# Zero pads written as 16 bit elements, and a new hand-held issue order, in a one-core linear attention and gated convolution kernel

## The chip, the cores and the metric

The kernel runs on one core of a Trainium2 chip. The metric is device microseconds of one execution. A core has a matrix engine (TensorE, PE in the profile), three elementwise engines (VectorE or DVE, ScalarE or ACT, GpSimd or POOL), a queue engine (SyncE, SP) and 16 DMA engines. Each engine takes its instructions strictly in its own order; engines meet through semaphores.

## The reference, cut to what matters

For 8 batches, 8 heads, 576 positions and a head size of 64, a linear attention is computed, its output is laid out as (position, 512), and a gated convolution follows:

```python
r = np.maximum(x, 0.0)                       # phi for q and k
phi = np.concatenate([r * cos_w, r * sin_w], axis=-1)
kv  = einsum('bhsf,bhsd->bhfd', k_p, v);  z = sum(k_p, axis=2)
att = einsum('bhsf,bhfd->bhsd', q_p, kv) / (einsum('bhsf,bhf->bhs', q_p, z) + 1e-06)
x1, x2, x3 = split(att @ w_proj)             # 512 -> 3 * 512
x2_conv = irfft(rfft(x2) * rfft(filter_fft)) # over the 576 positions
out = (x1 * x2_conv * x3) @ w_out            # 512 -> 512
```

## The kernel before

Everything is held in fp16 with fp32 accumulation in PSUM. One batch is one pass through these named steps; a step is a Python generator, and each `yield` in it ends one piece:

- `Lq`, `Lk`, `Lv` (line 278 and 285) load a batch of q, k or v from HBM into one of six `raw` tiles over POOL's DMA queue, as two transfers: partitions 0 to 63 take five positions each, partitions 64 to 127 take four. `Sk` loads the first half of k of batch 0 over SP's queue into a tile that shares its memory with `att`. Half 0 and 1 of batch 0 are loaded apart. `Lw`, `Lf`, `Lo` load `w_proj` in three thirds, the filter and `w_out`.
- Since the upper 64 partitions have four positions and the lower have five, the fifth place of the upper ones is zeroed once in each `raw` tile: `pad:0` to `pad:5` (step_pad, line 358), on DVE. `pd32` does it for the fp32 tile (line 362).
- `cols`, `rows`, `tf`, `ti`, `th`, `io`, `id`, `sine`, `zero` build the tables of sines and masks. `ccol`, `scol`, `tcol` are the weights of phi.
- `pk`, `pq`, `va` make phi(k), phi(q) and the scaled v, in pieces on DVE (line 249) or ACT (lines 605 and 477). `kv` (line 654) and its eviction `kvs`, `qt` (transposes of q: on PE, line 675, for batches 0 to 2, as DMA transposes on SP, line 666, from batch 3), `num` (line 689, then `rcp` at line 699 and `att` on DVE), `xp` or `xt` (transposes of `att`, line 721 on PE, line 711 on SP).
- `ga` and `gb` are the x1 and x3 matmuls with `w_proj` (line 858), evicted to `x0s` and `x2s`, multiplied in `g`. `bf`, `pr`, `dm`, `dr`, `dl`, `xe`, `pd`, `inv`, `y` are the convolution by a factored transform (lines 769 to 895). `out` (line 937 and 943) is the last product; its result is scaled into one of three `os` tiles (line 268) and stored by SP (lines 969 and 959).

No scheduler orders the work: `PLAN` is a text of words such as `pq:0.1'a*3`, each word advances one step by one piece (`*3`: three pieces; `'a`: this piece on ACT, `'v`: on DVE, in place of the step's own engine), and each engine gets its instructions in the order of the text. A `~` ahead of a load holds it until the last scalar or tensor operation that DVE had been given in the text is done. `UNITS` is a text of digits: which of the four PSUM tiles each new unit takes. Waits between engines are derived by the framework from the tiles that instructions read and write. POOL builds the descriptors of its transfers itself, some 0.65 to 0.75 us for each.

step_pad writes its zeros through an fp32 view of the fp16 tile:

```python
nc.vector.memset(raw_buf[i].bitcast(FP32)[64:128, :, 2 * D : 5 * D // 2], 0.0)
```

Of the kernel before, what the change touches and what calls it, by code (L numbers as in the profile page):

```python
# [10 lines left out]
FP32 = mybir.dt.float32  # L11
# [16 lines left out]
    num:0.1 rows: va:0.1 pq:0.1'a pk:0.1*2 num:0.0 num:0.1 pq:0.1 num:0.1 tf:0 qt:0.2 num:0.0  # L28
    pk:0.1'a tf:1 qt:0.3 rows: va:0.1 num:0.1 rows: pk:0.1 pq:1.2 pk:0.1'a qt:0.2 kv:0.1
    pq:1.2'a num:0.0 kv:0.1 ~Lw:0.0.4 pq:1.2'a qt:0.3'v xp:0.0*2 ti: pq:1.2 num:0.2 num:0.3  # L30
    pq:1.2 num:0.2 tf:0 pq:1.2 num:0.2 num:0.3 va:1.2'v qt:1.3 Lk:1.2 num:0.3 qt:1.2 va:1.2'v
    num:0.2 num:0.3 qt:1.3'v qt:1.0 qt:1.2 xp:0.1 Lw:1.0.4 va:1.2 ti: xp:0.1'v gb:0.1 qt:1.0
    qt:1.1 bf:0.0 ti: bf:0.1 gb:0.0 bf:0.0 gb:0.0 va:1.2'v qt:1.1'v tf:0 gb:0.1 Lv:2.2 ga:0.1*2
# [12 lines left out]
    pd:0.1 pq:3.2 gb:1.2 kv:2.2 gb:1.1 num:2.0 bf:1.0 qt:2.3 pd:0.0 gb:1.1 gb:1.2 bf:1.1 gb:1.1
    inv:0.3 num:2.0 pq:3.2*2 gb:1.2 num:2.0 inv:0.3 inv:0.1 num:2.0 g:1.1 inv:0.2 bf:1.1 inv:0.1
    inv:0.2 bf:1.1 num:2.1*2 gb:1.3 num:2.1 pq:3.2 va:3.2 gb:1.3 inv:0.0 gb:1.3 bf:1.0 Lk:4.2
    pr:1.1 num:2.1 pq:4.2 g:1.2 inv:0.0 xp:2.0 bf:1.1 num:2.2 bf:1.0 y:0.5 pr:1.1 num:2.2
    num:2.3 va:3.2 y:0.5 xp:2.0 num:2.2 pq:3.2'a pr:1.1 bf:1.1 pq:3.2'a bf:1.0 pq:4.2 pr:1.0*2  # L50
    va:4.2 num:2.3 num:2.2 pr:1.2 num:2.3 pk:3.2 pr:1.2 ga:1.3*2 num:2.3 xp:2.1 pr:1.0 dm:1.1
    va:3.2'v pq:4.2 ga:1.3 bf:2.0 dm:1.0 xp:2.1 dr:1 ga:2.0 y:0.5*2 ga:2.0 pk:3.2 y:0.4 xe:1.0
    pk:3.2 va:3.2'v Lo: y:0.5 y:0.4 dl:1 ga:2.0 xe:1.2 gb:2.1 gb:2.0 va:4.2'v xe:1.1 y:0.4*2
    g:1.3 ga:2.1 gb:2.1 y:0.4 bf:2.1 pk:3.2 pd:1.2 gb:2.0 ga:2.1 bf:2.0 qt:3.2 va:3.2 gb:2.1
    out:0.1 pd:1.2 Lv:5.2 gb:2.0 pk:3.2'a*2 gb:2.2 pd:1.2 out:0.1 bf:2.1 g:2.0 kv:3.2 bf:2.0
    pd:1.2*2 kv:3.2 ~Lq:5.2 va:4.2 ga:2.1 qt:3.1 out:0.1 pk:4.2 gb:2.2 qt:3.3 ga:2.2 kv:3.2
    bf:2.1*2 bf:2.0 ga:2.2 gb:2.2 bf:2.1 out:0.2 bf:2.0 va:4.2 pk:4.2 g:2.1 inv:1.0 pq:4.2
# [12 lines left out]
    inv:2.1'v inv:2.2 y:2.4 num:4.1 qt:5.0 inv:2.3 inv:2.2 pr:3.0 num:4.1 y:2.4 inv:2.3 pk:5.2'a  # L70
    pr:3.1 va:5.2 num:4.1 gb:3.2 y:2.4 pr:3.1 pk:5.2'a num:4.1 num:4.2 pr:3.0'v kv:5.2*2 g:3.1
    bf:3.2 gb:3.2 qt:5.1 pr:3.1 y:2.4 y:2.5 num:4.2 y:2.5 kv:5.2 pr:3.2 num:4.2 num:5.0 y:2.4
    gb:3.2 num:4.2 dm:3.1 pr:3.2 num:5.0 num:5.3 num:5.0*2 dm:3.0 num:5.3 dr:3 num:5.3*2
    ga:3.3*2 va:6.2'v y:2.5 gb:3.3 xe:3.1 gb:3.3 xe:3.0 xt:4.0 ga:3.3 xt:4.1 gb:3.3 pk:6.2 y:2.5
    qt:5.2 num:5.1 dl:3 ~Lq:6.2 num:5.1 xe:3.2 num:5.1 g:3.2 pd:3.2 ga:4.0 gb:4.0 num:5.1 ga:4.1
    ga:4.0 y:2.5 pd:3.2 gb:4.0 va:6.2 ga:4.0 gb:4.0 ga:4.1 g:3.3 num:5.2 out:0.1 bf:4.2 gb:4.1
    out:2.0 num:5.2 g:4.0 num:5.2*2 gb:4.1 out:2.0 gb:4.2 ga:4.1 xt:5.0 gb:4.1 pd:3.2*2 gb:4.3
    bf:4.2 gb:4.2 bf:4.2*2 ga:4.2 ~Lq:7.2 out:2.0 g:4.1 gb:4.2 pd:3.2 gb:4.3*2 ga:4.3*2 ga:4.2
    pq:6.2 ga:4.3 inv:3.2 xt:5.1 inv:3.3 inv:3.0 ga:4.2'v g:4.3 inv:3.3 out:1.0 inv:3.2 bf:4.2
    inv:3.1 pk:6.2'a g:4.2 out:2.0 pk:6.2 bf:4.2 bf:5.2 out:1.2 ga:5.1 pr:4.0 pq:6.2 pk:6.2  # L80
    pk:6.2'a ga:5.1 inv:3.1 y:3.5 pr:4.0 bf:4.2 pr:4.1*2 y:3.5 inv:3.0 va:6.2 out:2.1 bf:4.2
# [6 lines left out]
    bf:5.2 gb:5.0 out:3.1 gb:5.0 inv:4.1 qt:6.0 bf:5.2 inv:4.2 pk:7.2 y:4.4 gb:5.0 y:4.4 num:6.1
    inv:4.2 num:6.1 pr:5.2 out:3.2 y:4.4 pr:5.2 qt:6.2 qt:6.3 num:6.1 g:5.1 gb:5.3 num:6.0
    out:3.2 va:7.2 g:5.0 gb:5.3 num:6.1 num:6.0 gb:5.3 ga:5.3*2 num:6.2 num:6.0*2 inv:4.3 ga:5.3  # L90
    pk:7.2 pr:5.1 num:6.3 num:6.2 inv:4.3 pr:5.1 num:6.2 y:4.4 num:6.2 num:6.3 gb:5.2*2 num:6.3
    va:7.2'v num:6.3 dm:5.0 pr:5.1 y:4.5*3 out:3.2 dm:5.1 dr:5 gb:5.2 dl:5 ga:5.2 xt:6.0 y:4.5
# [955 lines left out]
```

## Time and profile before

| what | value |
| --- | --- |
| median of 3 runs | 236.4 us (235.6 to 236.49) |
| the profiled execution | 235.66 us, of which the span of its instructions is 233.9 us |
| PE matmuls | 205.8 us busy, 88% of the span, 2260 instructions |
| DVE | 199.4 us busy, 85%, 573 instructions |
| ACT | 174.1 us busy, 74%, 266 instructions |
| POOL | 43.7 us busy, 19% |
| mean granted TensorE clock | 0.962 |

The profiled execution lies 0.74 us below the median, and 1.76 us of it are outside the span. Busy time merges overlapping instructions of an engine: a DVE instruction of 0.34 us may start 0.26 us after the one before. A matmul's end is modelled, so that a PE that is shown busy need not be at its peak. L numbers are lines of the kernel, and many share the line of a helper: L249 is any scalar operation on DVE, L254 any tensor operation, L268 any eviction on ACT.

### The profile page before, as it was taken

Reading aid. Unit: us, or ns where it says so; the run is one execution under the profiler, and the core shown is the slowest. Engines: PE = TensorE matmul, PEld = TensorE weight load, DVE = VectorE, ACT = ScalarE, POOL = GpSimd, SP = SyncE. Lnnn points to the kernel's source line nnn. Section 1 sums busy time; section 2 is a strip of 40 time slices with the busy share of each in tenths; the row PEclk is TensorE's granted clock in tenths of the full one; section 3 lists DMA queues with packets and bytes.
Section 4 is the critical chain, followed back from the end, with each engine's and each line's share of the span. In section 5 each row is a group of like instructions: output and inputs, shape, how many; then the busy total and the mean of one; then the engine's idle time right before and its main releaser. Section 6 shows DMA issues by size and latency. Waiting matters only on the chain.

```text
span 233.9 us, 5838 instructions
## 1 busy us (share of the span) xinstructions
PE 205.8 (88%) x2260; PEld 135.9 (58%) x2260; DVE 199.4 (85%) x573; ACT 174.1 (74%) x266; POOL 43.7 (19%) x80
## 2 busy tenths in 40 slices
PE   0380599999999999998699999999999999999990
...
DVE  1480889999999999989479999999999799989960
...
PEclk9998579999999999999799999999999999999996
...
GB/s 130 106 156 189 201 202 150 0 130 200 168 174 201 201 160 119 137 202 199 162 144 152 189 185 201 226 197 153 131 150 226 190 170 154 114 0 7 108 219 185
DMA packets 73115, 36.78 MB, mean 157 GB/s; under 512 B 41152, under 2 KB 68800, under 8 KB 73088
## 3 DMA queue, kind: packets, MB, share of 16 engines
...
q14 instruction: 10, 0.08, 0.1%
...
## 4 chain that ended last, share of the span: by engine, by line
PE 76%; DMA 7%; issue 5%; DVE 5%; ACT 4%; SPq 1%; ACTq 1%; POOL 0%; DVEq 0%; POOLq 0%
PE ps L858 27%; PE ps L769 12%; PE ps L937 8%; DMA out_dram<-os 4%; PE ps L689 4%; PE ps L654 4%; PE ps L891 3%; PE ps L895 3%; PE ps L791 3%; DMA raw<-in_q_dram 2%; PE ps L675 2%; PE ps L778 2%; PE ps L721 2%; PE ps L802 2%; ACT os L268 1%
## 5 line engine op out<-in xcount | busy, mean ns | idle before, releaser
L858 PE MATMUL ps<-xt,wp 128*128 128x320 f16 (+1 forms) x512 | 72.8, 289 | 0.0
L858 PEld LDWEIGHTS <-wp 128*128 128x128 f16 x512 | 48.3, 99 | 17.7 <-issue 2.5
L937 PE MATMUL ps<-wo,y 128*128 128x512 f16 x128 | 31.3, 379 | 0.0
L769 PE MATMUL ps<-wp,fo 128*128 128x512 f16 x128 | 31.1, 379 | 0.0
L268 ACT ACTIVATE os<-ps 128x1024 f32<-128x1024 f32 (+1 forms) x21 | 16.9, 812 | 12.7 <-PE ps L937 7.5
L254 DVE TENSOR_TENSOR att<-ps,rcp 128x640 f16<-128x640 f32 x32 | 25.9, 819 | 0.2
L268 ACT ACTIVATE x2f<-ps 128x1024 f16<-128x1024 f32 (+1 forms) x23 | 19.7, 873 | 7.3 <-PE ps L769 6.8
L689 PE MATMUL ps<-kvs,qpt 128*128 128x65 f16 x320 | 14.8, 197 | 10.6 <-DVE qpt L266 6.5
L268 ACT CAST x2s<-ps 128x576 f16<-128x576 f32 x29 | 18.5, 647 | 4.9 <-PE ps L858 2.7
L689 PEld LDWEIGHTS <-qpt 128*128 128x128 f16 x320 | 13.7, 100 | 13.8 <-DVE qpt L266 6.6
L268 ACT CAST x0s<-ps 128x576 f16<-128x576 f32 x29 | 18.4, 645 | 3.9 <-PE ps L858 2.9
L268 ACT CAST eq<-ps 128x576 f16<-128x576 f32 x28 | 17.1, 653 | 3.8 <-PE ps L895 3.6
L937 PEld LDWEIGHTS <-y 128*128 128x128 f16 x128 | 12.0, 98 | 13.0 <-DVE y L254 1.0
L268 ACT CAST xf<-ps 128x1024 f16<-128x1024 f32 (+1 forms) x21 | 16.0, 809 | 3.8 <-PE ps L802 3.4
L769 PEld LDWEIGHTS <-fo 128*128 128x128 f16 x128 | 11.9, 98 | 11.0 <-issue 0.4
L254 DVE TENSOR_TENSOR eo<-eq 128x512 f16<-128x512 f16 (+1 forms) x72 | 16.8, 285 | 0.5
L477 ACT ACTIVATE va<-raw,ccol 128x512 f16<-128x512 f16 (+1 forms) x25 | 17.1, 688 | 0.0
L891 PE MATMUL ps<-itab,yf 128*128 128x144 f16 x128 | 16.9, 229 | 0.0
L895 PE MATMUL ps<-itl,yf 128*128 128x288 f16 x64 | 16.9, 291 | 0.0
L278 POOL DMA_DIRECT2D raw<-in_q_dram x9 | 6.4, 708 | 51.6 <-ACT x2s L268 19.7
L254 DVE TENSOR_TENSOR g<-x0s,x2s 128x576 f16<-128x576 f16 x32 | 14.0, 444 | 1.6 <-ACT x0s L268 1.5
L254 DVE TENSOR_TENSOR eo<-xt 128x512 f16<-128x512 f16 (+3 forms) x44 | 15.1, 367 | 0.0
...
## 6 DMA issues: line engine op xcount, KB each, us to landing
...
```

The source lines that it names most:

```text
L254: last_dve[0] = nc.vector.tensor_tensor(out=out, in0=in0, in1=in1, op=op)
L268: return nc.scalar.copy(out=out, in_=in_) if mul is None else nc.scalar.mul(out=out, in_=in_, mul=mul)
L278: first = queue.dma_start(out=rw[0:64, to], in_=rows[:, :, 0 : NJ * D])
L477: return nc.scalar.activation(out=dst, in_=src, func=AF.Copy if bias is None else AF.Identity, scale=col, **({} if bias is None else {"bia ...
L654: nc.tensor.matmul(u[:, g, ds((h % 4) * 65, 65)], kp[:, h, j].rearrange("p a b -> p (a b)"), va[:, h, j, 0:65], start=(j == 0), stop=(j == ...
L689: nc.tensor.matmul(u[:, hh, ds(t * 65, 65)], qpt[:, h, ds(t * 128, 128)], kvs[:, h // 4, ds((h % 4) * 65, 65)], start=True, stop=True,)
L769: nc.tensor.matmul(u[:, x], fo[:, bl, c, x], wp[c], start=(c == 0), stop=(c == NC - 1),)
L791: nc.tensor.matmul(u[:, comp], tab[:, ds(128 * bl + 32 * comp, 128)], x2f[:, cl], start=True, stop=False,)
L858: nc.tensor.matmul(uf[:, ds(512 - 64 * NJ * (1 - hf), 64 * n)], wp16[:, i, ds(w * DM + c * 128, 128)], xi[:, hf, 0:n], start=(i == 0), sto ...
L891: nc.tensor.matmul(u[:, comp, ds(par * QS, QS)], yf[:, comp, ds(par * DM + c * 128, 128)], itab[:, par + 4 * comp], start=(par == 0), stop ...
L895: nc.tensor.matmul(u[:, comp, 0:HS], yf[:, comp, 2 * DM : NF], itl[:, c, comp].rearrange("p a b -> p (a b)"), start=False, stop=True,)
L937: nc.tensor.matmul(u[:, x], y[:, c, ds(128 * t, 128)], wo16[:, c], start=(c == 0), stop=(c == NC - 1),)
```

## The change

The zeros of step_pad are written through the tile's own 16 bit view. Both texts, `PLAN` and `UNITS`, are replaced: the order of the pieces, the engine of some, the places of the loads and of the holds, and the PSUM tile of each unit. Nothing else differs. Below: the edited line, the head of the two plans, and the stretch around the stores of batches 0 and 1.

```diff
     def step_pad(i):
-        nc.vector.memset(raw_buf[i].bitcast(FP32)[64:128, :, 2 * D : 5 * D // 2], 0.0)
+        nc.vector.memset(raw_buf[i][64:128, :, 4 * D : 5 * D], 0.0)
...
 PLAN = """
-    pad:3 pd32:0 Lq:0.0 io:1 Sk:0.0 io:2 zero: pad:1 pad:0 ~Lv:0.0 th: pk:0.0'a io:0 id: ~Lq:0.1
-    rows: cols: rows: zero: rows: pad:2 pq:0.0 Lv:0.1 id: cols: rows:*2 cols: pq:0.0 warm:0.12
-    th: rows: pq:0.0 th: pk:0.0*2 pq:0.0 rows: Lk:0.1 rows: th: pq:0.0'a ~Lq:1.2 va:0.0'v
-    pq:0.0'a va:0.0'v*2 rows: pad:4 tf:0 pk:0.0'a tf:1'v cols: va:0.0'v pq:0.1 pk:0.0 rows:
-    qt:0.0 tf:1 pk:0.0'a ones:0 va:0.0 io:3 Lv:1.2 ones:1 qt:0.1 pad:5 pq:0.1'a va:0.1'v
-    qt:0.1'v kv:0.0 pq:0.1'a qt:0.0 pq:0.1 sine: tf:0 pk:0.1 ~Lw:2.0.4 va:0.1*2 kv:0.0 num:0.0
+    io:1 pad:5 io:0 ~Lq:0.0 Sk:0.0 id: pd32:0 rows: pad:2 pad:1 zero: cols: ones:0 pk:0.0'a
+    cols: rows: Lq:0.1 cols: sine: rows: pk:0.0'a zero: Lv:0.0 rows:*2 id: pad:4 rows: ~Lk:0.1
+    io:2 pad:3 ~Lv:0.1 ~Lq:1.2 pad:0 rows: ~Lv:1.2 pk:0.0'a rows: pq:0.0 ones:1 pq:0.0'a*3
+    warm:0.12 pq:0.0'a pk:0.0 rows: th: tf:0 pq:0.0 pq:0.1 th: pq:0.1'a th: tf:1'v rows:
+    va:0.0'v io:3 qt:0.0 pq:0.1 pk:0.0 va:0.0'v qt:0.1 va:0.0*2 ~Lw:2.0.4 pk:0.0'a va:0.0
+    qt:0.0'v tf:0 pq:0.1'a pk:0.1 pk:0.1'a tf:1 qt:0.1 pk:0.1 kv:0.0 rows: kv:0.0 cols: pq:0.1
...
-    pr:2.1 num:3.0 inv:1.1 y:1.4 out:0.0 num:3.0 g:2.2 pr:2.2 pq:5.2'a out:0.0 out:0.2 pr:2.1
-    pr:2.2 dm:2.1 Lk:5.2 y:1.4 xt:3.1 dm:2.0 num:3.0 pk:4.2 y:1.4 qt:4.0 pq:5.2'a y:1.4 dr:2
-    out:0.0 xe:2.0 dl:2 xe:2.2 pq:5.2 qt:4.3 y:1.5 kv:4.2*2 y:1.4 out:1.0*2 xe:2.1 g:2.3 out:1.1
-    va:5.2 out:1.2 pk:5.2'a kv:4.2'v ~Lk:6.2 xt:3.0 pq:5.2 num:4.0 out:1.1 pd:2.2*3 num:4.0
-    out:1.2'v pq:5.2 bf:3.2 out:1.0 out:0.0 qt:4.1 num:4.0*2 bf:3.2 gb:3.0 pk:5.2'a ga:3.0
-    out:1.1 qt:4.2 gb:3.0 pd:2.2 ga:3.0 pd:2.2 gb:3.1 num:4.3 gb:3.1 bf:3.2 num:4.3 gb:3.0
+    y:1.5 pq:5.2 num:3.2 y:1.5 bf:2.0 pr:2.1 pq:4.2'a pq:5.2'a inv:1.1 out:0.0'v num:3.2 out:0.1
+    xt:3.0 pq:5.2 pr:2.1 pr:2.2 y:1.4 pr:2.2 dm:2.0 qt:4.3 dm:2.1 qt:4.0 va:4.2 dr:2 num:3.2
+    kv:4.2 y:1.4*3 va:5.2'v xe:2.1 dl:2 y:1.4 xe:2.0 xt:3.1 kv:4.2 ~Lk:6.2 out:1.1 kv:4.2
+    xe:2.2'v pd:2.2 out:1.0 pd:2.2 out:1.1 out:1.2 g:2.2 pq:5.2'a va:5.2 out:1.0 pk:5.2'a ga:3.0
+    out:1.2 bf:3.2 num:4.0 out:1.0 out:0.0 pd:2.2 bf:3.2*2 ga:3.0*2 gb:3.0*2 pd:2.2 num:4.0
+    pk:5.2 num:4.0 pq:5.2 num:4.0 out:1.1 num:4.3*2 pd:2.2 out:1.2 g:2.3 gb:3.1 pk:5.2'a num:4.3
...
```

More of the change, by code (lines that the diff above doesn't have):

```diff
@@ L28 @@
[L28 to L33, printed above, removed]
@@ L46 @@
[L46 to L51, printed above, removed]
@@ L52 @@
[L52 to L57, printed above, removed]
@@ L70 @@
[L70 to L75, printed above, removed]
@@ L76 @@
[L76 to L81, printed above, removed]
@@ L88 @@
[L88 to L92, printed above, removed]
-    ga:5.2 xe:5.0 xe:5.2 xt:6.1 pk:7.2 gb:6.1 xe:5.1 ga:6.0 y:4.4 out:3.0 g:5.3 ga:6.1 pk:7.2'a
@@ new lines @@
+    tf:1 rows: qt:0.3'v num:0.0 xp:0.0 Lv:2.2 rows: pq:1.2*3 Lf:1 qt:0.2 pq:1.2 kv:0.1 ti:
+    pq:1.2 num:0.3 num:0.2 pq:1.2 qt:1.0 ti: num:0.3 num:0.2 xp:0.0 num:0.3 num:0.2 qt:1.1
+    num:0.3 num:0.2 th: va:1.2 qt:1.3 bf:0.0 qt:1.0 qt:1.1 xp:0.1 xp:0.1'v gb:0.0 qt:1.2
+    va:1.2'v tf:0 va:1.2 gb:0.1 gb:0.0 bf:0.1 qt:1.3'v tf:0 gb:0.0 gb:0.1*2 bf:0.0 ga:0.1 bf:0.1
+    bf:0.0 ~Lf:0 tf:1 qt:1.2'v ga:0.1 ti: va:1.2'v ga:0.0 tf:0 bf:0.0 va:1.2'v bf:0.1 ga:0.0
+    ga:0.1 gb:0.3 bf:0.1 pk:1.2 gb:0.3 ga:0.0 gb:0.2 ga:0.3 pk:1.2 ga:0.3 pk:1.2*3 g:0.1
@@ new lines @@
+    xp:1.1'v pk:2.2 pq:2.2'a xe:0.1 ti:'v pq:2.2 pk:2.2'a h:1 ga:1.0 dl:0 h:1 bf:1.1 pk:2.2
+    gb:1.1*2 pd:0.1 h:2 ti:'v ga:1.0 pq:2.2'a pk:2.2'a gb:1.1 gb:1.0 bf:1.1 pk:2.2 h:2 pq:2.2
+    qt:2.1 xe:0.2 bf:1.0 pk:2.2 gb:1.0 gb:1.2 pd:0.1 ga:1.0 pd:0.1 gb:1.2 va:2.2'v bf:1.1 qt:2.2
+    bf:1.1 pd:0.0 gb:1.0'v va:2.2 qt:2.1 bf:1.0 kv:2.2 pq:3.2'a Lo: g:1.0 late: kv:2.2 qt:2.0
+    bf:1.1 qt:2.2'v pd:0.0 kv:2.2 qt:2.0 ga:1.1 gb:1.2'v ga:1.1*2 pd:0.1 num:2.1 pd:0.1 pd:0.0
+    Lq:4.2 num:2.1 bf:1.0 ga:1.2 va:3.2 inv:0.3*2 ga:1.2 inv:0.2 g:1.1 Lk:3.2 num:2.1 qt:2.3
@@ new lines @@
+    bf:2.1 pk:3.2 gb:2.1 xe:1.0 ga:2.1 ga:2.0 bf:2.1 ga:2.0 y:0.4 va:4.2 ga:2.1 xe:1.1 pq:4.2
+    gb:2.1 pk:3.2 y:0.4 ~Lq:5.2 ga:2.1 gb:2.0 pk:3.2 y:0.4 va:3.2'v dl:1 xe:1.2 gb:2.0 bf:2.0
+    out:0.1 out:0.2 ga:2.0 pd:1.2 pk:3.2'a bf:2.1 kv:3.2 out:0.1 pd:1.2 Lk:5.2 Lv:5.2 kv:3.2
+    bf:2.0*2 gb:2.0 pd:1.2 gb:2.3 g:2.1 pd:1.2 va:4.2 out:0.2 gb:2.3 pq:4.2'a pd:1.2 pk:4.2
+    kv:3.2 ga:2.2 qt:3.0 out:0.1 inv:1.3 gb:2.3 pq:4.2 g:2.0 inv:1.3 pk:4.2'a num:3.3*2 qt:3.2
+    bf:2.1 ga:2.2 inv:1.0 inv:1.2 bf:2.1 ga:2.2 num:3.3 inv:1.0'v va:4.2'v out:0.2 num:3.1
@@ new lines @@
+    inv:1.2 num:3.0 ga:2.3 num:3.0 num:3.3 ga:2.3 pr:2.0 num:3.1 bf:2.0 y:1.5 pr:2.0 num:3.1
+    bf:2.1 ga:2.3 pk:4.2'a num:3.1 out:0.2 gb:2.2 y:1.5 gb:2.2 num:3.0 pk:4.2'a pr:2.1 pk:4.2'a
+    pk:4.2 y:1.5 bf:2.0 gb:2.2 num:3.0 out:0.0 pr:2.0 num:3.2 bf:2.1 pq:4.2 out:0.0 inv:1.1
+    y:1.5 pq:5.2 num:3.2 y:1.5 bf:2.0 pr:2.1 pq:4.2'a pq:5.2'a inv:1.1 out:0.0'v num:3.2 out:0.1
+    xt:3.0 pq:5.2 pr:2.1 pr:2.2 y:1.4 pr:2.2 dm:2.0 qt:4.3 dm:2.1 qt:4.0 va:4.2 dr:2 num:3.2
+    kv:4.2 y:1.4*3 va:5.2'v xe:2.1 dl:2 y:1.4 xe:2.0 xt:3.1 kv:4.2 ~Lk:6.2 out:1.1 kv:4.2
@@ new lines @@
+    y:2.4 pr:3.0 pr:3.1 y:2.4 num:4.2*2 g:3.1 pr:3.0 va:5.2 gb:3.3 ga:3.2 num:4.2 num:4.1 pr:3.0
+    y:2.4 xt:4.1 y:2.5 gb:3.3 kv:5.2 gb:3.3 pr:3.2 kv:5.2 num:4.1*2 y:2.4 qt:5.1 num:4.1 y:2.5
+    pk:6.2 ga:3.3*2 y:2.5 va:6.2'v kv:5.2 pr:3.2 num:5.0 num:5.3 num:5.0 xt:4.0 num:5.3 num:5.0
+    dm:3.1 ga:3.3 num:5.3 dm:3.0 dr:3 qt:5.2 num:5.0 num:5.3 num:5.1 pk:6.2'a*2 xe:3.0 ~Lq:6.2
+    g:3.3 gb:3.2 xe:3.1 num:5.1*2 y:2.5 gb:3.2 dl:3 out:1.0 gb:4.0 num:5.1 gb:3.2 gb:4.0 pk:6.2
+    y:2.5 g:3.2 bf:4.2 gb:4.1 ga:4.1 xe:3.2 pd:3.2 gb:4.1 ga:4.1 gb:4.1 pd:3.2*2 out:2.0
@@ new lines @@
+    va:6.2'v ga:4.1 ga:4.0*2 pd:3.2 num:5.2*2 gb:4.0 ga:4.0 va:6.2 out:2.0 ga:4.3 num:5.2 xt:5.0
+    bf:4.2 ga:4.3 gb:4.3 va:6.2 out:2.0 num:5.2 g:4.1 gb:4.3*2 pd:3.2 xt:5.1 bf:4.2 ~Lv:7.2
+    ga:4.2*2 g:4.0 gb:4.2*2 inv:3.1 ga:4.3'v ~Lq:7.2 pk:6.2'a ga:4.2 ga:5.1 pq:6.2 gb:4.2
+    inv:3.0 out:1.2 inv:3.1'v inv:3.0 va:6.2 inv:3.2 inv:3.3 bf:4.2 ga:5.1 bf:4.2 pr:4.0 inv:3.3
+    pq:6.2 bf:4.2 bf:5.2 bf:4.2 inv:3.2 pr:4.1 pr:4.0 y:3.4 bf:4.2 g:4.3 pr:4.1 pk:6.2'a pr:4.0
+    y:3.4 pr:4.1 out:2.1 bf:5.2 pr:4.2 pq:6.2 out:2.2 y:3.4 ga:5.1'v bf:5.2 dm:4.0 va:7.2'v
@@ new lines @@
+    bf:5.2 out:2.1 out:2.2 y:3.4 y:3.5 bf:5.2 pr:4.2 out:2.1 dm:4.1 y:3.5 g:4.2 dl:4 dr:4 gb:5.1
+    pq:6.2 bf:5.2 xe:4.2 y:3.5 kv:6.2 xe:4.1 gb:5.1 y:3.5 xe:4.0 y:3.4 kv:6.2 pq:6.2'a gb:5.1
+    y:3.5 Lk:7.2 out:2.2*2 out:3.1 pr:5.0 pq:7.2'a va:7.2'v out:3.1 out:3.2 pd:4.2 out:2.0
+    out:3.2 pr:5.0 pd:4.2 pq:7.2 pq:6.2 g:5.1 out:1.1 out:3.1 pd:4.2 pk:7.2 pd:4.2 pk:7.2'a
+    out:3.0 qt:6.1 qt:6.0 kv:6.2'v out:3.0 gb:5.0 out:3.0 pd:4.2 inv:4.1 pr:5.0'v gb:5.0 inv:4.0
+    va:7.2'v num:6.1 bf:5.2 qt:6.3 inv:4.1 va:7.2'v gb:5.0 pq:7.2'a inv:4.0 num:6.1 ga:5.0
@@ new lines @@
+    inv:4.3 qt:6.2 ga:5.0 out:3.0 gb:5.2 num:6.1*2 ga:5.0 inv:4.2 num:6.0 y:4.4 g:5.0 y:4.4
+    gb:5.2 inv:4.3 inv:4.2 pk:7.2'a pr:5.1 y:4.4 num:6.0 y:4.4 va:7.2 num:6.0 bf:5.2 num:6.0
+    num:6.3 gb:5.2 y:4.5 pr:5.1 ga:5.3 out:3.2 xt:6.0 pr:5.1 pr:5.2 pq:7.2 ga:5.3 pr:5.2
+    pq:7.2'a num:6.3 y:4.5 num:6.3 num:6.2 dm:5.1 num:6.3 ga:5.3 gb:5.3 num:6.2*2 gb:5.3*2 y:4.5
+    dm:5.0 dr:5 num:6.2 y:4.4 xe:5.0 dl:5 ga:5.2*2 ga:6.1 pk:7.2 y:4.5 g:5.3 xe:5.2 xe:5.1 y:4.5
+    pq:7.2'a pd:5.2 gb:6.1 out:4.0 ga:5.2 out:4.0 xt:6.1 ga:6.1 gb:6.0 gb:6.1 gb:6.0 bf:6.2*2
```

89 lines of the change are left out of this document (40 added, 49 removed).

## The prediction

> **What bounds the kernel now.** I read the page first, for the span and the 40 slices (5.85 us each), then the time lines of DVE, ACT and PE at the start, then the waits, and last the stretch where the PE row dips a second time.
>
> ```profile
> span 233.9 us, 5838 instructions
> ...
> PE   0380599999999999998699999999999999999990
> ...
> DVE  1480889999999999989479999999999799989960
> ...
> PEclk9998579999999999999799999999999999999996
> ```
>
> PE is full from slice 6 to slice 38, but for a notch in slices 18 and 19 (105 to 117 us). Its empty part is the first 35 us. From 40 to 100 us DVE is busy 9.5 to 10.0 of every 10 us and ACT 9.65 to 10.0 as well, so that there three engines are full at once, and no order of the same work can gain much. Gains lie at the start, in the notch and at the end. The DVE line of the start:
>
> ```profile
> 1.65 0.27 DVE L358 MEMSET raw<- 64x256 f32 x1
> 7.83 0.27 DVE L358 MEMSET raw<- 64x256 f32 x1 [5.91 <-DMA raw<-in_q_dram]
> ...
> 16.36 0.47 DVE L366 TENSOR_SCALAR va<-ccol 128x80 f16<-128x80 f32 x2
> 24.14 0.27 DVE L358 MEMSET raw<- 64x256 f32 x1 [7.31 <-DMA raw<-in_v_dram]
> ```
>
> Two pads of 0.27 us each wait 5.91 and 7.31 us for a transfer into the same `raw` tile. The load never touches the bytes that the pad writes (it fills four places of the upper partitions, the pad the fifth); a pad whose load comes ahead of it in the plan is made to wait all the same. Everything on DVE queues behind it, and ACT and PE wait for what is queued:
>
> ```profile
> 25.93 0.54 ACT L413 ACTIVATE fsin<-tn_fwd,m_pi 128x288 f16<-128x288 int32 x1 [6.63 <-DVE tn_fwd L407]
> ```
>
> ```profile
> 16.60 0.80 PE L654 MATMUL ps<-va,kp 128*128 128x65 f16 x20 [0.62 <-DVE va L366]
> ...
> 25.52 0.73 PE L689 MATMUL ps<-kvs,qpt 128*128 128x65 f16 x10 [6.51 <-DVE qpt L266]
> ...
> 28.91 1.31 PE L654 MATMUL ps<-va,kp 128*128 128x65 f16 x20
> ```
>
> The same 20 matmuls cost 0.80 us before the stop and 1.31 us after it. The notch:
>
> ```profile
> 111.86 1.02 ACT L268 ACTIVATE os<-ps 128x1024 f32<-128x1024 f32 x1 [4.21 <-DMA out_dram<-os]
> ```
>
> ```profile
> 112.94 0.47 PE L689 MATMUL ps<-kvs,qpt 128*128 128x65 f16 x10 [2.97 <-ACT os L268]
> 113.25 2.50 PE L858 MATMUL ps<-xt,wp 128*128 128x320 f16 x12
> ```
>
> The eviction of `out:1.1` needs the `os` tile that `out:0.0` is stored from; that store was issued at 103.9 and landed at 111.8. PE stood 2.97 us, and its next 12 gate matmuls took 2.34 us on the chain of waits, where 12 take 1.47 elsewhere.
>
> **The pads themselves.** In the built program the new pads are still 64x8x32 elements, as before, so 6 x 0.27 us stay. The row that shows why: the `warm` tile of 512 fp16 zeros appears as 128x256 uint32 and took 0.27 us, as the fp32 pads did. The Trainium skill (VectorE: DVE Perf Modes, section on zero memsets issued as uint32) says that a memset takes a cycle per element of whatever type, and that zeros of 16 bits can be issued as 4 byte words; the trace agrees. What changes is the wait: in the order of the built program no pad waits for a transfer any more.
>
> **The head, walked along ACT**, which after the change has the longest chain there. Before, ACT first sits until 7.26 us (k over SP), loads a table (1.28), does relu of k (1.27), loads a second table (1.28), and only then makes `ccol`, which `tcol` and every scaled piece wait for. After, the table for Sin is loaded first, `ccol` follows (0.30 after `io:0`, about 4.9 us), and no second load is in the program: -1.28. From the landing of k, unchanged at 7.2 us: relu 1.27, to 8.5. Then up to the first `kvs`: 13 pieces of 128x256 at about 0.42 us from start to start (5.5), three table pieces (1.45), 0.1, one `qpt` eviction (1.15) and `kvs` (0.35): 17.0 us, before 18.5. Up to the second `kvs`: five pieces and two table pieces (3.1), `qpt` (1.15), `kvs` (0.35): 21.6 us. Before, that second `kvs` ended at 30.6. So 9.0 us are gained, 7.3 of them the stall of `pad:5`, the rest the table and the earlier `ccol`. From there to the first gate matmul before took 4.8 us (35.43 - 30.63: `num`, `rcp`, `att`, `xp`, evictions), so it moves from 35.4 to 26.4.
>
> Do the loads follow? `Lq:0.0` is now behind eight iotas on POOL (some 1.5 us later: it starts at 2.75 and should land at 9.2 by the 5.7 us it took), and ACT wants it at 9.4. From then on nothing on POOL waits for DVE as it did (2.6 and 1.4 us), so `Lw:2` is issued at about 14.0 in place of 17.5. Before, it landed at 26.6, which is the need of after even if nothing came earlier; k of batch 1 landed at 32.5, and its first use moves from 41.2 to about 32.7. If the loads land 1.5 us later than before, the gain is 7.3 or so, and two such waits in a row take 3 from 8.5 and leave 5.5. The DMA share is 1.27 to 1.31 from 15 to 35 us, so the loads are near what this queue gives. I take 8.5, between 5.5 and 9.5.
>
> PE's clock: the granted clock is 0.67 and 0.50 in 20 to 30 us, after the idle 6.5 us. In my walk PE has no gap over 3 us after the `warm` matmuls. The Trainium skill (TensorE: Matmul & The Clock Gate, Part 1) puts the fall to half clock at one idle window of some 3.4 us; by that rule the head would stay fast. The notch's 2.97 us were already enough for a slow stretch here, so I add nothing for it.
>
> **The notch.** SP's order is still transposes, then the store of `out:0.0`. But `out:0.0` is evicted by DVE and early, the two `qt` ahead of the last `xt` are issued before its `att` is there, and ACT has 5.9 us of work between the last `xf` and the eviction that waits, against 4.5. With two `xf` ahead (2 us), ACT arrives 8 us after the `att`; the store lands 1.7 + 7.5 = 9.2 us after it. So ACT waits about 1.2 us in place of 4.2. Bounds: nothing gained, or all of 2.97 plus the slow matmuls behind it on the chain of waits (2.34 for 1.47, 0.96 for 0.49 of `inv`, 1.31 for 0.98: 1.7 us), 4.6. I take 3, the wait's own difference.
>
> **Engine choice.** Counting both programs and pricing by rows, DVE gains two evictions of 128x1024 (2 x 1.22), one `qpt` (0.81), one `kvs` (0.70), three gate evictions (2.24), three `va` (1.02), two small `xf` (0.85), two smaller ones (1.1), and loses two `xf` (2.43), seven `pk` (2.4) and four `pq` (1.9): +2.4 us. ACT comes out at -0.3. DVE has 18 us of idle time behind 35 us, most of it in the notch and at the end, but only 0.8 from 40 to 100. The cost lies between 0 and 2.4; I take 2. PE's sequence is the same work in nearly the same order: the first matmul of each step of each batch moves by under 2.5 us of PE work in nearly all cases. The last stores share the three `os` tiles as before: 0, give or take 1.
>
> **Sum.** 235.66 - 8.5 - 3 + 2 = 226.2 for an execution like the profiled one, which lies 0.74 under its median: 227.0.
>
> **Rivals.** (1) The stall moves from the pad to real loads: DVE now meets `pq:1.2`, `pk:1.2` or the weights before they land, the notch stays, DVE pays in full: -5.5 + 0 + 2.4, or 233.3. For it speaks the DMA share, against it that DVE shows no wait for a load but at the pads. 231 to 233.5. (2) The change doesn't do what it says: pads still wait, and only the order of the rest moves; 236. Against it: the built program names no such wait. (3) Slower: SP issues in order, so that a `qt` or `xt` that waits for PE or `att` holds the stores behind it, ACT stands at an `os` eviction, its PSUM tile stays taken, and PE stops and goes cold. Before, it happened once, at the border of batches 1 and 2, for 4.6 us. There are five more such borders where stores stand between transposes. With the notch unmended, one new stop leaves -8.5 + 2 + 4.6 = -1.9, and two give -8.5 + 2 + 9.2 = +2.7, or 239.1: it is slower from the second on. For it: 20 `qt` and 10 `xt` on the same queue as 47 stores. Against: before, ACT waits for a store at one of the 21 `os` evictions of L268. (4) Better: the head's 9.5, the notch's 4.6, DVE's surplus hidden and the end 1 shorter: 221.3 or less.
>
> **How the numbers follow.** Forecast 0.69 (221.5 to 230); rival 1 0.15; rival 2 0.03; rival 3 0.08; rival 4 0.05. The range 221.5 to 233.5 holds the first two, 0.84; its ends are about the sums of the bounds, -9.5 - 4.6 - 1 and -5.5 + 0 + 2.4, from 236.4. A difference under 0.5% (1.2 us) could not be told from none here. Faster 0.69 + 0.15 + 0.05 = 0.89, same 0.03, slower 0.08.
>
> **What would show it.** Right: no wait at L358; one table load; the second `kvs` near 22 us and the first L858 near 26.5; ACT's longest wait for a store about 1 us, and no clock under 0.9 near 105. Wrong: DVE waits of over 2 us at L249 for `raw`; L858 waiting for `wp`; a first gate matmul after 30 us; a PE gap of over 2 us behind 40 us; DVE busy above 202 with an idle PE beside it.

## The result, and the profile after

The changed kernel takes 225.05 us (median of 4, 224.68 to 225.53), beside 236.3 us for the kernel before on the same chip: 0.953 of its time, 95% interval 0.950 to 0.956. The profiled execution took 224.68 us with a span of 222.9, so its span is 11.0 us shorter. Of two experiments below (the ninth and the tenth) the profiled execution was 1.5% or more longer than the shortest of its own runs; their rows say what waits, and the lengths read from them need not hold for other executions. All ratios are to the kernel before on the same chip.

The page of the kernel after, in 40 slices of 5.57 us:

```profile
span 222.9 us, 5833 instructions
...
PE   0958999899999999998999999999999999999970
...
DVE  4799999999999999999889999998979999899960
...
PEclk9999999999999999999999999999999999999996
```

Counted from 0, PE is now full from slice 4 to slice 37, but for an 8 in slice 7, where before it was full from slice 5 on; of the notch of slices 18 and 19 an 8 in slice 18 is left, and the granted clock never falls before the last slice. DVE's line of the start, with the two last pads and the piece behind them:

```profile
6.72 0.55 DVE L358 MEMSET raw<- 64x256 uint32 x2
7.89 0.49 DVE L249 TENSOR_SCALAR qp<-raw 128x1280 f16<-128x1280 f16 x1 [0.18 <-DMA raw<-in_q_dram]
```

A pad is still 64x256 words and 0.27 us. No pad has a bracket with a DMA any more; DVE's first wait for a load is the 0.18 us of a `pq` piece that really reads it. ACT and then PE, the head's path (start, duration, and in brackets the idle time before it and what ended it):

```profile
2.91 1.28 ACT L387 ACT_TABLE_LOAD   x1 [2.91 <-DVE half_pi L374]
6.01 1.27 ACT L605 ACTIVATE kp<-att 128x1280 f16<-128x1280 f32 x1 [1.40 <-DMA att<-in_k_dram]
14.92 0.37 ACT L268 CAST kvs<-ps 128x260 f16<-128x260 f32 x1
19.20 0.38 ACT L268 CAST kvs<-ps 128x260 f16<-128x260 f32 x1
```

```profile
15.34 0.77 PE L689 MATMUL ps<-kvs,qpt 128*128 128x65 f16 x20 [1.50 <-ACT kvs L268]
...
17.55 0.94 PE L654 MATMUL ps<-va,kp 128*128 128x65 f16 x20 [0.32 <-DVE att L254]
...
24.21 0.65 PE L858 MATMUL ps<-xt,wp 128*128 128x320 f16 x4
```

One table load, the second `kvs` done at 19.6 instead of 30.6, the first gate matmul at 24.21 instead of 35.43; PE's 6.51 us of idle time is 1.50. At the notch, ACT's line and SP's:

```profile
102.03 1.02 ACT L268 ACTIVATE os<-ps 128x1024 f32<-128x1024 f32 x1 [1.25 <-DMA out_dram<-os]
```

```profile
93.14 1.36 SPq L711 DMA_TRANSPOSE xt<-att  x1
94.56 1.40 SPq L969 DMA_DIRECT2D out_dram<-os  x2
```

The eviction waits 1.25 us where it waited 4.21. The store is still behind the `xt`, issued at 94.6 and landed 7.4 us later, at 102.0. Counted from the issue of that `xt` (101.9 before, 93.1 now), ACT comes after 7.6 us in place of 5.8 and the store lands after 8.8 us in place of 9.9: 1.9 of the 3.0 us are ACT's later arrival, 1.1 the earlier landing. What the whole gain is made of is read from three stretches, bounded by the first gate matmul (L858) and by the first `dm` matmul (L791) of batches 2 and 4. The busy times of the stretches between, before and then after (length, then PE, PE loads, DVE, ACT, POOL busy, granted clock, DMA share, GB/s):

```profile
35.43:99.70 64.27, 64.27 (x815) 45.05 (x814) 63.47 (x202) 63.30 (x96) 16.91 (x23) 1.00 1.04 148
```

```profile
24.21:90.95 66.74, 65.65 (x817) 45.17 (x814) 65.58 (x201) 62.32 (x93) 15.80 (x24) 1.00 1.20 178
```

The head gave 11.2 us. The next 64 us became 2.5 longer, with DVE 2.1 us busier and idle for only 1.2. The stretch around the notch (99.70 to 150.46 before, 90.95 to 138.42 after) went from 50.76 to 47.47, -3.3. The rest of the batches to the end went from 83.44 to 84.48, +1.0. -11.2 + 2.5 - 3.3 + 1.0 = -11.0.

### The profile page after: what moved, and what is told of

The parts are those of the page before. It is cut to its first block, busy times and chain, and to the rows that moved or that the text cites. A ratio compares the mean times of both kernels' runs of the same rounds, so it can differ in the third digit from the quotient of the medians.

```text
span 222.9 us, 5833 instructions
## 1 busy us (share of the span) xinstructions
PE 204.3 (92%) x2260; PEld 133.0 (60%) x2260; DVE 203.4 (91%) x574; ACT 173.4 (78%) x264; POOL 42.7 (19%) x80
## 4 chain that ended last, share of the span: by engine, by line
PE 50%; DVE 25%; ACT 13%; issue 5%; DMA 4%; ACTq 1%; SPq 0%; DVEq 0%
PE ps L858 19%; PE ps L769 8%; PE ps L937 6%; DVE att L254 4%; DVE eo L254 4%; DVE y L254 3%; DVE yf L254 3%; PE ps L891 3%; PE ps L689 3%; PE ps L895 3%; PE ps L654 2%; ACT kp L605 2%; ACT qp L605 2%; DVE qp L249 2%; DMA att<-in_k_dram 2%
## 5 line engine op out<-in xcount | busy, mean ns | idle before, releaser
L858 PE MATMUL ps<-xt,wp 128*128 128x320 f16 (+1 forms) x512 | 72.3, 286 | 0.4 <-DVE att L254 0.2
L858 PEld LDWEIGHTS <-wp 128*128 128x128 f16 x512 | 48.0, 98 | 17.5 <-issue 2.8
L769 PE MATMUL ps<-wp,fo 128*128 128x512 f16 x128 | 30.2, 379 | 0.0
L268 ACT CAST x2s<-ps 128x576 f16<-128x576 f32 x28 | 17.8, 642 | 6.2 <-PE ps L858 5.7
L268 ACT ACTIVATE os<-ps 128x1024 f32<-128x1024 f32 (+1 forms) x18 | 14.4, 810 | 9.3 <-PE ps L937 4.9
L268 ACT CAST eq<-ps 128x576 f16<-128x576 f32 x28 | 17.7, 647 | 4.3 <-PE ps L895 4.1
L268 ACT CAST x0s<-ps 128x576 f16<-128x576 f32 x27 | 17.2, 642 | 4.7 <-PE ps L858 4.5
L937 PEld LDWEIGHTS <-y 128*128 128x128 f16 x128 | 11.9, 97 | 13.2 <-DVE y L254 0.9
L769 PEld LDWEIGHTS <-fo 128*128 128x128 f16 x128 | 12.1, 97 | 12.3 <-issue 0.4
L268 ACT CAST xf<-ps 128x1024 f16<-128x1024 f32 (+1 forms) x21 | 17.4, 862 | 1.9 <-PE ps L802 1.2
L689 PE MATMUL ps<-kvs,qpt 128*128 128x65 f16 x320 | 14.1, 194 | 1.6 <-ACT kvs L268 1.5
L689 PEld LDWEIGHTS <-qpt 128*128 128x128 f16 x320 | 13.1, 98 | 4.1 <-issue 1.9
L605 ACT ACTIVATE kp<-raw,tcol 128x512 f16<-128x512 f16 (+1 forms) x22 | 14.9, 695 | 0.0
```

Source lines behind the costliest of these rows:

```text
L268: return nc.scalar.copy(out=out, in_=in_) if mul is None else nc.scalar.mul(out=out, in_=in_, mul=mul)
L605: nc.scalar.activation(out=dst, in_=src, func=AF.Relu, **({} if col is None else {"scale": col}))
L689: nc.tensor.matmul(u[:, hh, ds(t * 65, 65)], qpt[:, h, ds(t * 128, 128)], kvs[:, h // 4, ds((h % 4) * 65, 65)], start=True, stop=True,)
L769: nc.tensor.matmul(u[:, x], fo[:, bl, c, x], wp[c], start=(c == 0), stop=(c == NC - 1),)
L858: nc.tensor.matmul(uf[:, ds(512 - 64 * NJ * (1 - hf), 64 * n)], wp16[:, i, ds(w * DM + c * 128, 128)], xi[:, hf, 0:n], start=(i == 0), sto ...
L937: nc.tensor.matmul(u[:, x], y[:, c, ds(128 * t, 128)], wo16[:, c], start=(c == 0), stop=(c == NC - 1),)
```

## The experiments

**The view alone, in the kernel before.**

```diff
-        nc.vector.memset(raw_buf[i].bitcast(FP32)[64:128, :, 2 * D : 5 * D // 2], 0.0)
+        nc.vector.memset(raw_buf[i][64:128, :, 4 * D : 5 * D], 0.0)
```

> The kernel before with one line changed: the pads are written through the 16 bit view, the plan stays. Theory (the false wait is most of the head's gain): both DVE waits at L358 go; pad:5's 7.3 us come off the first gate matmul in full, and pad:0's wait frees the loads that POOL held for DVE, but ACT still loads two tables and makes ccol at 11 us, so the first L858 comes at 27.5 to 28.5 us in place of 35.4 and the time is 228 to 230. Rival A (real loads take the wait over): DVE or PE waits for raw or wp, first L858 after 31 us, time above 232. Rival B (the new order of the head is what gained, the waits were covered): 235 to 236.

229.03 us, ratio 0.974 (0.970 to 0.979): 6.4 us below the 235.46 of the kernel before on that chip. The first gate matmul starts at 27.90. Of the two pads that waited before, `pad:0` is now the second of a pair that starts at 1.66 us, and `pad:5` stands here, both with no wait:

```profile
16.90 0.27 DVE L358 MEMSET raw<- 64x256 uint32 x1
```

So one line of the diff carries more than half of the gain, under the old plan.

**The new plan with the old view.** The same line the other way round, in the kernel after.

> The kernel after with only the pads put back to the fp32 view. In the new plan only pad:0 stands behind loads of its own tile (both halves of q of batch 0), so only it can wait. Theory (a pad is made to wait only where its load is ahead of it in the plan): one DVE wait at L358, from about 7.0 us to the landing of the second half of q near 9.2 us, 1 to 2.3 us, first L858 at 25 to 26.5 and time 226 to 227.4. Rival (the view is worth the whole gain in any order): first L858 beyond 30, time above 231.

227.64 us, 0.970 (0.964 to 0.975). The plan (`PLAN` and `UNITS` together; no run separates them) without the view is worth about as much as the view without the plan (the intervals overlap), and it too takes most of the pads out of the loads' way: one is left behind its load. DVE's line of that pad:

```profile
9.25 0.27 DVE L358 MEMSET raw<- 64x256 f32 x1 [2.25 <-DMA raw<-in_q_dram]
```

One false wait of 2.25 us remains, and the first gate matmul is at 26.75, 2.5 us later than in the kernel after. Not all of that need be the wait: in this execution the granted clock was 0.50 from 15 to 20 us, where the kernel after has 1.00, and the second `kvs` waits 0.56 us for PE.

**The old view, all pads moved ahead of every load, in the kernel before.**

```diff
-    pad:3 pd32:0 Lq:0.0 io:1 Sk:0.0 io:2 zero: pad:1 pad:0 ~Lv:0.0 ...
+    pad:3 pad:1 pad:0 pad:2 pad:4 pad:5 pd32:0 Lq:0.0 io:1 Sk:0.0 io:2 zero: ~Lv:0.0 ...
```

> The kernel before, fp32 view kept, with all six pads moved to the front of the plan, ahead of every load. Theory (what costs is the pad's place behind its load, whatever the view): the same as the 16 bit view alone within 0.5 us, 228 to 230.5, the 1.1 us of memsets ahead of the masks costing next to nothing since k lands at 7 us anyway. Rival (the fp32 view itself is slow or waits anyway): 234 to 236.

228.89 us, 0.973 (0.969 to 0.977), first gate matmul at 27.92: the same as the view alone, within 0.2 us. The fp32 memset isn't dearer than the 16 bit one (six of them took 1.64 us in a row here). What costs is its place behind a load of the same tile together with the other view: with the 16 bit view the pad at the same place in the plan does not wait. Either cure is enough.

**The view, and the tables of the first columns ahead of k's relu, in the kernel before.**

```diff
-    pad:3 pd32:0 Lq:0.0 io:1 Sk:0.0 io:2 zero: pad:1 pad:0 ~Lv:0.0 th: pk:0.0'a io:0 id: ~Lq:0.1
-    rows: cols: rows: zero: rows: ...
+    pad:3 pd32:0 Lq:0.0 io:1 Sk:0.0 io:2 io:0 zero: cols: pad:1 pad:0 ~Lv:0.0 th: pk:0.0'a id: ~Lq:0.1
+    rows: rows: zero: rows: ...
```

> The kernel before with the 16 bit view and, besides, io:0, zero and cols moved ahead of the first relu of k on ACT, so that the table for Sin is loaded before k lands and ccol is made early. Theory (ACT's chain sets the head once the pads are free): 1.28 us of table load and about 1.3 to 2.5 us of waiting for ccol go, first L858 2 to 3 us ahead of the one with the view alone, time 1.5 to 3 us below it, 226 to 228. Rival (loads or DVE set the head by then): less than 0.7 us below it.

225.81 us, 0.960 (0.956 to 0.963): another 3.2 us. The first gate matmul is at 25.27. With the view and two moved words (`io:0` and one `cols`) the old plan is about 1 us from the new one (1.1 by the spans, 0.8 by the medians, 1.6 by the ratios). Behind the head it has the old plan's lengths: 64.30 us up to the notch (64.27 before), 50.80 around it (50.76). So everything else in the new plan, its 3.3 us at the notch included, comes to about 1 us net.

**The store of `out:0.0` on SP ahead of the transposes, in the kernel before.**

```diff
-    va:5.2 out:1.2 pk:5.2'a kv:4.2'v ~Lk:6.2 xt:3.0 pq:5.2 num:4.0 ...
-    out:1.2'v pq:5.2 bf:3.2 out:1.0 out:0.0 qt:4.1 ...
+    va:5.2 out:1.2 pk:5.2'a kv:4.2'v ~Lk:6.2 out:0.0 xt:3.0 pq:5.2 num:4.0 ...
+    out:1.2'v pq:5.2 bf:3.2 out:1.0 qt:4.1 ...
```

> The kernel before with one move: the store of out:0.0 is issued on SP ahead of the transpose xt:3.0 in place of behind it. Theory (the notch comes from the store standing behind transposes on SP's queue): store issued about 1.7 us earlier, ACT's wait at the eviction of out:1.1 falls from 4.2 to 2.5 us or less, PE's stop from 3.0 to 1.3 or less, time 1.5 to 3.5 us less, 233 to 235. Rival A (the wait is the DMA engines' load, not the place in the queue): the store lands at the same time, no change. Rival B (xt:3.0 is now late): PE or DVE waits for xt, time up to 1 us more.

241.0 us, 1.019 (1.011 to 1.026): 4.5 us slower. ACT's wait for the store did fall, to 1.3 us. In the list of waits (total, times, longest) stands what came in its place:

```profile
DVE eo L254 <- DMA xt<-att: 8.1, 1, 8.1
PE ps L858 <- DMA xt<-att: 8.0, 1, 8.0
...
ACT os L268 <- DMA out_dram<-os: 2.1, 2, 1.3
```

The transpose behind the store landed 12.1 us after its issue, PE waited 8.0 us for it, and the granted clock fell to about a half for two slices. The rival that named this was right, and far too small.

**The same store issued by ACT, right after the eviction, in the kernel before.**

```diff
-                nc.sync.dma_start(
+                (nc.scalar if b == 0 and grp == 0 else nc.sync).dma_start(
```

> The kernel before with the store of out:0.0 issued by ACT right behind its eviction, so that it stands behind no transpose on SP's queue. Theory: issued near 101.5 and 102, landed by 106, ACT does not wait at the eviction of out:1.1 (it came there at 107.6 before), PE has no stop over 1 us near 110 and its clock stays at 1.0; ACT pays about 1 us for issuing. Time 2.5 to 4.5 us less, 231.5 to 233.5. Rival (DVE is the bound through that stretch, PE's stop is covered by its work): less than 1.5 us.

239.59 us, 1.012 (1.005 to 1.019): 3.1 us slower. SP's order is no longer in the way, ACT does not wait for the store, and still:

```profile
PE ps L858 <- DMA xt<-att: 5.1, 1, 5.1
```

The transpose lands 11.4 us after its issue here, 12.1 behind the store on SP's queue, and 3.7 in the kernel before, where the store comes after it. So the queue that issues the store isn't what delays the transpose; the store and the load of k, which POOL issues at 103 us, run beside it. The Trainium skill (DMA: Bandwidth & Descriptors, section on issuing engines not being separate DMA queues) says that transfers started by any engine run on the same 16 DMA engines and interleave. The two runs agree with it, with waits of 8.0 and 5.1 us.

**Two evictions put back from DVE to ACT, in the kernel after.**

```diff
-    ... dm:1.1 num:2.3 bf:2.0 pr:1.2'v y:0.4
+    ... dm:1.1 num:2.3 bf:2.0 pr:1.2 y:0.4
...
-    ... inv:1.1 out:0.0'v num:3.2 out:0.1
+    ... inv:1.1 out:0.0 num:3.2 out:0.1
```

> The kernel after with two evictions put back from DVE to ACT: the 512 wide x2f of batch 1 and the 1024 wide os of out:0.0, 1.9 us of DVE by their rows, in the stretch from 67 to 91 us where DVE is busy 98% and ACT has 3.7 us idle. Theory (DVE's work sets that stretch): 1 to 1.9 us less, 223 to 224. Rival (the evictions were moved because ACT came late to what PE or a store waits for): no change or up to 2 us more, with the wait at out:1.1's eviction back near 3 us.

226.93 us, 0.960 (0.955 to 0.965), not faster. DVE is less busy up to the notch (64.82 us in 24.86 to 91.90, in place of 65.58) and the stretch is 0.3 us longer, not shorter. ACT's line of the waiting eviction:

```profile
103.80 1.02 ACT L268 ACTIVATE os<-ps 128x1024 f32<-128x1024 f32 x1 [1.79 <-DMA out_dram<-os]
```

It is 1.8 us later than in the kernel after, and the stretch that holds it, from one batch's first `dm` matmul to the next, is 0.8 us longer. So these two moves, which the prediction counted only as a load on DVE, about pay for themselves on ACT. Another 0.65 us of the 2.0 between the spans lies at the start, where the programs are the same.

**Five pieces of `pk` and `pq` of batch 2 put from ACT to DVE, in the kernel after.**

```diff
-    ... xe:0.0 ti:'v h:0 pq:2.2'a h:0 ...
-    xp:1.1'v pk:2.2 pq:2.2'a xe:0.1 ti:'v pq:2.2 pk:2.2'a h:1 ...
-    gb:1.1*2 pd:0.1 h:2 ti:'v ga:1.0 pq:2.2'a pk:2.2'a gb:1.1 ...
+    ... xe:0.0 ti:'v h:0 pq:2.2 h:0 ...
+    xp:1.1'v pk:2.2 pq:2.2 xe:0.1 ti:'v pq:2.2 pk:2.2 h:1 ...
+    gb:1.1*2 pd:0.1 h:2 ti:'v ga:1.0 pq:2.2 pk:2.2 gb:1.1 ...
```

> The kernel after with all five pieces of pk:2.2 and pq:2.2 that it gives to ACT done by DVE: 5 x 0.27 us more on DVE, 5 x 0.62 less on ACT, between 40 and 60 us where both are over 98% busy. Theory (DVE sets the stretch, and its surplus costs in full): 1 to 1.6 us more, 226 to 226.7. Rival (ACT sets it): 1 to 3 us less.

227.7 us, 0.963 (0.957 to 0.969). The stretch from the first `dm` matmul of batch 0 to that of batch 1:

```profile
40.40:68.69 28.29, 26.43 (x372) 18.35 (x369) 28.25 (x86) 24.41 (x34) 6.59 (x10) 1.00 1.13 160
```

It took 28.29 us with DVE busy 28.25; in the kernel after it is 27.15 with 27.05. DVE's added 1.2 us came out as 1.14 us of time: here DVE is the bound, not ACT, which fell from 26.94 to 24.41 and brought nothing. By the ratios the whole kernel is 2.4 us slower than the kernel after; the profiled execution is the shortest of its four (226.02 of 226.02 to 228.34), so what the others add to the 1.14 us is not shown.

**The fourth experiment, with the load of k of batch 6 behind the notch.** Two edits of the head and one word moved.

```diff
-    va:5.2 out:1.2 pk:5.2'a kv:4.2'v ~Lk:6.2 xt:3.0 pq:5.2 ...
+    va:5.2 out:1.2 pk:5.2'a kv:4.2'v xt:3.0 pq:5.2 ...
...
-    ... pd:2.2 ga:3.0 pd:2.2 gb:3.1 num:4.3 ...
+    ... pd:2.2 ga:3.0 pd:2.2 gb:3.1 ~Lk:6.2 num:4.3 ...
```

> The kernel before with the 16 bit view and the early cols (as in the fourth run, 225.8 us), and the load of k of batch 6 moved some 10 us later in the plan, behind the eviction of out:1.1; the rest of the plan stays. In the runs so far this load (issued within 0.5 us of the store of out:0.0) runs beside the store and the transpose xt:3.0, and one of the two lands 6 to 9 us after its issue. Theory (three transfers share the DMA engines there, and the late one is what the notch waits for): without the load the store lands in 4 to 5.5 us, ACT's wait falls from 5.8 to under 2 us, PE's for xt from 2.7 to under 0.5, and the time by 1.5 to 3 us, to 222.8 to 224.3. Rival (the transposes alone hold the store): both waits stay within 1 us of what they were, no change of time.

225.28 us, 0.951 (0.946 to 0.956), which can't be told from the kernel after (0.950 to 0.956). The median lies outside the 222.8 to 224.3 that was expected. The notch itself is gone in the trace: the stretch that took 26.9 us in the fourth experiment takes 23.6, with no wait for `xt` or a store. But the next one, 23.9 there, takes 28.5 in this execution, the longest of the six:

```profile
127.76 1.02 ACT L268 ACTIVATE os<-ps 128x1024 f32<-128x1024 f32 x1 [3.76 <-DMA out_dram<-os]
```

The same wait for a store stands one batch further on. Single runs went from 222.71 to 226.58 us, so this need not come in each of them.

**The same load moved in the kernel after.**

```diff
-    ... y:1.4 xe:2.0 xt:3.1 kv:4.2 ~Lk:6.2 out:1.1 kv:4.2
+    ... y:1.4 xe:2.0 xt:3.1 kv:4.2 out:1.1 kv:4.2
...
-    ... out:1.1 num:4.3*2 pd:2.2 out:1.2 ...
+    ... out:1.1 num:4.3*2 ~Lk:6.2 pd:2.2 out:1.2 ...
```

> The kernel after with the load of k of batch 6 moved behind the eviction of out:1.1, some 7 us later. Theory: the store of out:0.0 lands in 4 to 5.5 us in place of 7.4, ACT's 1.25 us wait and PE's 0.9 us of gaps near 103 go, time 0.3 to 1.2 us less. Rival (DVE's work sets this stretch, or the load is then missed later): 0 to 1 us more.

230.82 us, 0.975 (0.969 to 0.980), some 5 us slower than the change. ACT no longer waits for the store at the notch, but two other waits do not fit:

```profile
DVE va L249 <- DMA raw<-in_v_dram: 5.8, 2, 5.6
...
PE ps L689 <- DMA qpt<-qp: 5.2, 1, 5.2
```

k is issued at 103.5, in place of 94.9, and v at 107.9, so that both loads now run beside the four `qt` transposes that SP issues from 100.8 on. v's second transfer took 13.3 us to land. k wasn't missed; v and the transposed q were. So moving this load cost 5 us in one plan and changed little in the other (0.960 to 0.951, intervals that touch).

**The first load of q ahead of the iotas on POOL, in the kernel after.**

```diff
-    io:1 pad:5 io:0 ~Lq:0.0 Sk:0.0 id: ...
+    Lq:0.0 io:1 pad:5 io:0 Sk:0.0 id: ...
```

> The kernel after with the first load of q issued ahead of the eight iotas, without a hold, as the kernel before has it. Theory (in the kernel after k landed at 5.9 us in place of 7.2 because q's transfer no longer ran beside it): k lands near 7 us again, ccol comes 0 to 0.7 us later, ACT's chain and the first L858 move by 0.8 to 1.3 us (25.0 to 25.5), time 0.5 to 1.3 us more. Rival (k's landing is chance, or q being there earlier makes up for it): first L858 within 0.3 us of 24.2, no change.

227.29 us, 0.963 (0.959 to 0.968), about 2.4 us slower. q was issued 0.9 us earlier; k's relu, which starts between 5.77 and 6.36 us in every other run of this plan, starts at 6.94 after a wait for its transfer, and the table load, behind work of DVE that waits for POOL's iotas, is 1.7 us later, at 4.64. The first gate matmul is at 26.57, after this wait:

```profile
26.57 0.66 PE L858 MATMUL ps<-xt,wp 128*128 128x320 f16 x4 [1.13 <-DMA wp<-in_moe_w_proj_dram]
```

POOL's later loads, held for work of DVE that needs the iotas, moved back too: the weights are issued at 15.1 in place of 13.2.

**One warming matmul in place of twelve, in the kernel after.**

```diff
-    warm:0.12 pq:0.0'a pk:0.0 rows: th: ...
+    warm:0.1 pq:0.0'a pk:0.0 rows: th: ...
```

> The kernel after with one warm matmul in place of twelve (the others' results are never read). Theory (the head's chain runs over ACT and DVE, and PE's clock matters little before the gates): the transposes and kv of batch 0 run at half speed, 20 transposes in 2.1 us in place of 1.3, first L858 0.3 to 1.2 us later, PE at full clock by 30 us, time 0.3 to 1.5 us more. Rival (the sparse head never brings the clock up, and the first gates run at half speed too): 2 to 4 us more, granted clock below 0.8 until 30 us.

226.94 us, 0.962 (0.959 to 0.967), some 2 us slower. The first gate matmul is at 25.34. Four executions with the twelve and with the same head have it at 24.21 (the kernel after), 24.57, 24.86 and 25.41, so the head's own part is 0 to 1.1 us. The latest of the four is the tenth experiment, where the clock fell all the same:

```profile
10.00:15.00 5.00, 2.46 (x41) 1.99 (x40) 4.72 (x18) 5.00 (x11) 5.00 (x12) 1.00 1.17 145
15.00:20.00 5.00, 4.09 (x60) 3.96 (x59) 3.58 (x11) 4.79 (x11) 2.73 (x4) 0.66 1.35 188
```

The other 1.0 us of its span lies behind the head, 0.6 of it between the first `dm` matmuls of batches 3 and 4, and 0.2 in each of two later batches; no run here tells what of it is the spread between executions.

## Why the prediction was right, point by point

The forecast was 227.0 us; 225.05 was measured, inside the range and on the side of the head. For the profiled execution 226.2 was forecast (with the 0.74 that makes 226.9) and 224.68 measured. The head brought 2.7 us more than forecast, the notch, the engines and the end together 1.2 us less; that these offset each other in part was luck.

**Pads.** Right: the same 0.27 us each, and only the waits gone. The first and third experiment settle that the wait, not the write, was the cost.

**Head.** The mechanism was right, the walk along ACT too, but the term was mis-sized: 8.5 taken, 11.2 measured. The walk itself gave 9.0, of which 0.5 was given away for loads that might come late; none made an engine wait for over 0.6 us (`Lw:2` was issued at 13.2, forecast 14.0). Of the other 2.2 us, 1.2 come from the line "from the landing of k, unchanged at 7.2 us": it landed at 6.0. The eleventh experiment shows a cause: q's load, which the new plan holds behind the iotas, is issued 0.9 us later and so runs beside it for a shorter time. I had priced that move as a delay of q alone. The last 1.0 are the three legs of the walk, 9.3, 4.3 and 4.6 us in place of 9.8, 4.6 and 4.8: the pieces follow each other at 0.40 us, not 0.42, other steps are shorter than their rows' durations, since an instruction starts up to 0.1 us before the one ahead of it ends, and the last leg was priced in a head whose granted clock was 0.81 (30 to 35 us). By the first gate matmul of single executions, the view brought 7.5 us (35.43 to 27.90), the early table and `ccol` 2.6 (to 25.27) and the rest of the plan 1.1 (to 24.21), where the walk had 7.3 for the stall and 1.7 for the table and `ccol`.

**Clock.** The kernel after has a warm head, as forecast, with a granted clock of 1.00 in each stretch of 5 us from 10 to 210. But the reason given, that PE has no gap over 3 us, does not decide it. In the tenth experiment, with the same head, the clock fell to 0.66 in 15 to 20 us with no PE gap over 1.51 us after the first matmuls, and in the second and fourth, with other heads, to 0.50 and 0.76 with none over 1.14 and 1.47 us. From 10 to 15 us PE was busy 2.46 us in the tenth, 3.42 in the second and 2.99 in the fourth; in the kernel after it was busy 2.96 us, and the clock stayed. So the same head may fall into either case, and that it stayed warm here was in part luck; what decides is not shown. The Trainium skill (TensorE: Matmul & The Clock Gate, Part 1) has half clock after an idle window of some 3.4 us, in a window that runs free of the program. These three executions do not agree with the idle window.

**Notch.** Right in size, 3 against 3.3, and in detail: 1.2 us of wait forecast, 1.25 measured. Counted from the issue of the last `xt`, the store lands after 8.8 us (forecast 9.2) and ACT comes after 7.6 (forecast 8), so both were 0.4 too long and the difference right. The 7.5 us in that 9.2 were read from the second half of the store alone, issued at 104.3 in the kernel before; from the issue of the first, at 103.6, it was 8.2. The prediction gave nothing to the store's place on SP's queue; the fifth and sixth experiment bear this out from the other side: an earlier store costs 3 to 5 us.

**Engine choice.** +2 forecast, +2.5 measured up to the notch. The count behind it was short: by the two pages DVE is busy 4.0 us longer (199.4 to 203.4), not 2.4, and 2.1 of it lies between the first gate matmul and the notch. So the prediction's sign of DVE above 202 us came true, but with little idle PE beside it, 1.1 us up to the notch. The eighth experiment shows DVE as the bound from 40 to 69 us. But the seventh shows that the surplus isn't one term: two of the moved evictions bring on ACT about what they cost.

**End.** 0, give or take 1, forecast; +1.0 measured behind the first `dm` matmul of batch 4. Half of it comes ahead of that of batch 7, where PE is shown busy throughout in both kernels, half behind it. No experiment took it apart; it stays open.

**Rivals.** The stall did not move to real loads (rival 1): the longest wait of DVE for a load is 0.6 us. No wait at L358 is left (rival 2). No new stop of PE at an `os` eviction came up (rival 3), but a new wait of ACT did, as its line in the list of waits shows (total, times, longest):

```profile
ACT os L268 <- DMA out_dram<-os: 2.9, 2, 1.7
```

The second one, of 1.7 us near 166 us, is longer than the wait of about 1 us that the prediction allowed; PE is busy throughout that batch (22.62 of 22.62 us from 158.85 on), so it cost PE nothing there. Still, the fifth, sixth, ninth and tenth experiments each brought on a new stop of PE by moving a single transfer, of 8.0, 5.1, 2.1 and 5.2 us: the price of 4.6 us was of the right size. Rival 4 had the head too small at 9.5.
